# A new table of places for all operations, and ten dummy matmul groups instead of four, in a fused linear-attention and feed-forward kernel

## The chip, the cores and the metric

The kernel runs on one core of one Trainium2 chip. TensorE (PE) multiplies, VectorE (DVE) and ScalarE (ACT) do the elementwise work, GpSimd (POOL) a few reductions across partitions, and SyncE (SP) issues every DMA from one queue, in order. The metric is the device time of one execution in microseconds (us); a kernel's time is the median of several runs.

## The reference, cut to what matters

```python
# q, k, v: 8 x 8 x 576 x 64 (batch, heads, sequence, head width), float32
q_s = softmax(q, axis=-1)                  # over the 64 of a head
k_s = softmax(k, axis=2)                   # over the sequence
kv  = einsum('bhsd,bhse->bhde', k_s, v)    # 64 x 64 for each head
x   = einsum('bhsd,bhde->bhse', q_s, kv)   # -> 4608 tokens x 512
h   = x @ w_in                             # 512 x 2048
g   = h * sigmoid(1.702 * h)
out = g @ w_out                            # 2048 x 512
```

Everything is float32. The weights arrive as 64-bit words and are converted on the chip.

## The kernel before, in words

The 4608 tokens are cut into twelve blocks of 384. A block needs its slice of x: DVE and ACT form the two softmaxes (lines 577 to 612 for the keys, 709 to 732 for the queries), PE multiplies keys with values (`kv_pairs`, line 643), transposes the queries against an identity (`q_tr`, 753) and multiplies both (`x_pairs`, 825). ACT and DVE bring x from PSUM to SBUF. For block 0 PE itself helps to form the low part of x (line 799).

To keep float32 accuracy, every operand of the feed-forward part is split into a high and a low part, and every product is three matmuls: high by high, high by low, low by high. Blocks 0 and 1 do this plainly: `g1` (line 853, x by w_in) and `g2` (line 885, g by w_out). The later blocks go in pairs: x and w_in are cut into quarters, from which seven products (`product`, line 1251, six matmuls of 384 columns each) give the eight quarter products. The same is done for w_out in the last four pairs (`stream`, `still_part`, both with matmuls of 256 columns at line 1386, and `gather`, which adds up the pieces); the pair of blocks 2 and 3 uses `out_part` (line 1514).

SBUF doesn't hold all the weights in all their forms. In the first 130 us the kernel loads the raw weights (`load_w`, line 419), converts them (`conv_w`: ACT at 448 and 463, DVE at 452, 456 and 473), and stores the results to DRAM tensors (`dwi`, `dwo`, later `dsh`, `dsl`, `dwa`, `dwb`). From then on `refill` (line 925) brings them back, half a megabyte at a time, into a few buffers that are used again and again: a load can be issued once the last matmul that reads the old contents has run, and it must land before the first matmul that reads the new. Two buffers, called wi4 and wi5 in the code, hold `dsh` and `dsl` pieces in turn. Early on, some weight buffers hold keys, values and queries of batches 0 and 1 (`ek`, `ev`, `eq`, `en`), and the raw weights that belong there wait until these have been read.

What sets the order: each operation is given to a `Plan` with its engine, what it reads and writes, and a closure that emits it. The table `FIRST` (line 115) has one number for each operation, its place in one list of all of them; operations are handed out so that each engine keeps the order of that list, and the program's instructions stand on each engine in that order. An engine runs its instructions strictly in order, so an instruction whose input is late holds up all that stand behind it on that engine; the same is true of SP, where a load whose buffer isn't free holds up the loads behind it.

At line 1596 `warm` emits a dummy group: two matmuls of the identity with itself into PSUM bank 3. Their result is never read (bank 3 is overwritten with `start=True` by the next user). Each dummy group is an operation of its own in the plan, so the table sets where it stands. It needs nothing but the identity, the second load of SP's queue.

Of the kernel before, what the change touches and what calls it, by code (L numbers as in the profile page):

```python
# [17 lines left out]
class Plan:  # L18
# [277 lines left out]
def efficient_attention_then_gelu_ffn(  # L296
# [1259 lines left out]
    def at(rank, f, *a):  # L1556
        tasks.append((rank, len(tasks), f, a))
# [43 lines left out]
    for i in range(4):  # L1601
        at(-89.05 + 0.001 * i, lambda rank: plan.add("PE", 0.93, ("ident",), (("bank", 3),), rank, warm))
# [256 lines left out]
```

## Time and profile before

| | us |
|---|---|
| median of 3 runs | 864.79 (863.8 to 866.38) |
| the profiled execution | 859.32, with a span of 857.5 |
| PE busy | 809.0 (94%), of it weight loads beside matmuls 755.1 |
| DVE busy | 607.0 (71%) |
| ACT busy | 488.6 (57%) |
| mean granted clock of TensorE | 0.994 |

The span runs from the first to the last instruction; 1.8 us of the profiled execution lie around it. Matmuls are pipelined, and a matmul's record holds its latency too, so PE's busy share is high wherever matmuls follow each other: what one costs is read from start to start in a stretch without waits. DMA was moving 268 GB/s on average, and at its highest some 420 GB/s.

### The profile page before, as it was taken

What the parts mean: (1) busy time and instruction counts of PE and PEld (TensorE: products, weight loads), DVE (VectorE), ACT (ScalarE), POOL (GpSimd) and SP (SyncE); (2) the same over time, 40 slices, a digit from 0 to 9 for tenths busy, and PEclk for the clock granted to TensorE, in tenths of its full rate; (3) what the DMA queues carried; (4) which work ended last, traced back from release to release, by engine and by line L of the source; (5) the groups of instructions that cost most, each with busy time, mean ns of one, the idle gap of its engine ahead of it and who ended that gap; (6) DMA issues with size and microseconds to landing.
All of it is one profiled execution on the core that took longest, in us unless ns stands there. A gap on an engine that the chain in (4) does not pass through costs nothing.

```text
span 857.5 us, 14803 instructions
## 1 busy us (share of the span) xinstructions
PE 809.0 (94%) x5716; PEld 755.1 (88%) x5716; DVE 607.0 (71%) x1091; ACT 488.6 (57%) x897; POOL 22.7 (3%) x21
## 2 busy tenths in 40 slices
PE   3799999999989999999999899999999999999998
PEld 2688988788878888989999889899999999899997
DVE  7898768787778787766786756887656476444474
ACT  3886456465645676656565564676565465335452
POOL 1100010000000100000000100000000000000000
PEclk9899999999999999999999999999999999999999
DMA  9878976627898879797877679757776668676763
GB/s 359 348 301 293 419 309 247 223 75 274 270 352 289 292 277 341 259 357 241 299 255 272 218 239 354 274 186 254 253 238 223 225 228 302 244 258 233 272 225 143
DMA packets 83190, 229.79 MB, mean 268 GB/s; under 512 B 8240, under 2 KB 32944, under 8 KB 83120
## 3 DMA queue, kind: packets, MB, share of 16 engines
q1 hardware_dynamic: 83120, 228.85, 74.4%
q8 instruction: 45, 0.74, 0.3%
q14 instruction: 25, 0.20, 0.1%
HBM read 181.63 MB, written 47.19 MB: 267 GB/s over the span
## 4 chain that ended last, share of the span: by engine, by line
PE 68%; DMA 19%; DVE 8%; ACT 2%; SPq 1%; issue 1%; DVEq 0%; ACTq 0%
PE bank L1251 26%; PE bank L1386 21%; PE bank L885 6%; PE bank L853 6%; PE bank L1514 5%; DMA w<-dwo 3%; DMA w<-dwi 2%; PE bank L643 2%; DMA dwb<-sl 2%; DMA w<-dsl 2%; DMA w<-dwa 2%; PE bank L825 1%; DMA kt<-in_k 1%; DMA w<-dsh 1%; PE bank L753 1%
## 5 line engine op out<-in xcount | busy, mean ns | idle before, releaser
L1251 PE MATMUL bank<-xc,w 128*128 128x384 f32 x1680 | 317.7, 338 | 15.0 <-DVE g L1270 4.0
L1251 PEld LDWEIGHTS bank<-xc,w 128*128 128x128 f32 x1680 | 289.1, 188 | 23.1 <-DVE g L1270 5.0
L1386 PE MATMUL bank<-w,pu 128*128 128x256 f32 x1260 | 167.6, 283 | 2.9 <-DMA w<-dwo 2.9
L1386 PEld LDWEIGHTS bank<-w,pu 128*128 128x128 f32 x1260 | 159.5, 189 | 7.4 <-issue 4.5
L1386 PE MATMUL bank<-w,xc 128*128 128x256 f32 x756 | 101.8, 282 | 2.4 <-DMA w<-dwb 1.2
L1386 PEld LDWEIGHTS bank<-w,xc 128*128 128x128 f32 x756 | 95.6, 188 | 4.8 <-ACT work L1476 1.4
L853 PE MATMUL bank<-xh,w 128*128 128x384 f32 x256 | 71.1, 342 | 1.4 <-ACT g L859 1.4
L885 PE MATMUL bank<-w,gh 128*128 128x512 f32 x192 | 61.1, 399 | 0.0
L853 PEld LDWEIGHTS bank<-xh,w 128*128 128x128 f32 x256 | 47.5, 191 | 3.8 <-ACT g L859 1.9
L1293 ACT COPY g<-bank 128x384 f32<-128x384 f32 x52 | 24.9, 479 | 41.0 <-PE bank L1251 35.6
L853 PE MATMUL bank<-xl,w 128*128 128x384 f32 x128 | 43.5, 340 | 0.0
L1278 ACT ACTIVATE g<-bank 128x384 f32<-128x384 f32 x51 | 25.0, 490 | 28.7 <-PE bank L1251 25.8
L1293 ACT COPY bank<-bank 128x384 f32<-128x384 f32 x40 | 18.6, 465 | 39.4 <-PE bank L1251 39.3
L885 PEld LDWEIGHTS bank<-w,gh 128*128 128x128 f32 x192 | 34.9, 188 | 6.3 <-issue 0.9
L1270 DVE TENSOR_TENSOR g<-bank,g 128x384 f32<-128x384 f32 x33 | 18.4, 556 | 28.0 <-PE bank L1251 25.9
L885 PE MATMUL bank<-w,gl 128*128 128x512 f32 x96 | 37.9, 395 | 0.0
L1289 DVE TENSOR_TENSOR pu<-g,pu 128x384 fp32r<-128x384 f32 x47 | 25.9, 562 | 16.7 <-ACT pu L1286 16.5
L591 POOL PARTITION_ALL_REDUCE mx<-mx x16 | 22.0, 1394 | 524.4 <-DVE mx L587 515.4
L1289 DVE TENSOR_TENSOR xc<-g,xc 128x384 fp32r<-128x384 f32 x32 | 17.7, 554 | 18.3 <-ACT xc L1286 18.3
L1514 PE MATMUL bank<-w,gp 128*128 128x512 f32 x108 | 29.7, 395 | 0.0
L859 ACT ACTIVATE g<-bank 128x384 f32<-128x384 f32 x32 | 15.5, 492 | 23.1 <-PE bank L853 21.8
L1293 ACT COPY work<-bank 128x384 f32<-128x384 f32 x28 | 13.4, 478 | 25.6 <-PE bank L1251 21.3
(187 smaller groups left out, 1308.9 us busy)
## 6 DMA issues: line engine op xcount, KB each, us to landing
w<-dwo SPq DMA_DIRECT2D x48, 512.0 KB, 5.5
w<-dwb SPq DMA_DIRECT2D x48, 512.0 KB, 6.9
w<-dwi SPq DMA_DIRECT2D x44, 512.0 KB, 5.9
w<-dsh SPq DMA_DIRECT2D x32, 512.0 KB, 5.2
w<-dsl SPq DMA_DIRECT2D x32, 512.0 KB, 5.6
w<-dwa SPq DMA_DIRECT2D x32, 512.0 KB, 6.1
vt<-in_v SPq DMA_DIRECT2D x14, 650.0 KB, 8.3
kt<-in_k SPq DMA_DIRECT2D x14, 640.0 KB, 5.9
```

Of the source, the lines that this page charges most:

```text
L591: nc.gpsimd.partition_all_reduce(flat, flat, P, bass_isa.ReduceOp.max)
L643: nc.tensor.matmul(pk[r0 : r0 + D, m // 2, m % 2], kt[:, o + a, c, :], vt[:, o + a, c, :], start=c == 0, stop=c == CM - 1, tile_position=( ...
L853: nc.tensor.matmul(ph, wi[w][j][:, c, :], x[:, c, :], start=c == 0 and i == 0, stop=c == KC - 1 and i == 2,)
L859: nc.scalar.activation(gt, ph, AF.Gelu_apprx_sigmoid)
L885: nc.tensor.matmul(po[c], x[:, cs], wo[w][j], start=j == 0 and i == 0, stop=j == NJ - 1 and i == 2)
L1251: nc.tensor.matmul(pb, ws[w][:, c * P : (c + 1) * P], xx[x][:, c * TB : (c + 1) * TB], start=p in FRESH and c == 0 and i == 0, stop=c == 1 ...
L1270: lambda: nc.vector.tensor_tensor(out=d, in0=pb, in1=o, op=ALU.add),
L1278: lambda: nc.scalar.activation(d, src, AF.Gelu_apprx_sigmoid), table="gelu")
L1289: lambda: nc.vector.tensor_tensor(out=get()[1], in0=d, in1=get()[0].bitcast(F32), op=ALU.subtract),
L1293: plan.add("ACT", act(TB), (PB,), (key,), free_, lambda: nc.scalar.copy(dst, pb))
L1386: nc.tensor.matmul(po, y[:, cs], w, start=start and i == 0, stop=i == 2, skip_group_check=True,)
L1514: nc.tensor.matmul(po[:, f0:f1], x[:, cs], w[:, h * DM + f0 : h * DM + f1], start=m == 0 and e == 0 and i == 0, stop=m == NQ - 1 and e == ...
```

## The change

The table `FIRST` is replaced as a whole (3222 numbers instead of 3216), and the loop that adds dummy groups runs ten times instead of four. No operation of the real work is added, removed or altered: the numbers of real DMAs, DVE, ACT and POOL operations are the same.

```diff
 FIRST = [
-    1870, 1, 3, 65, 33, 49, 51, 52, 4, 2, 0, 10, 9, 7, 6, 12, 22, 15, 110, 19, 115, 5, 31, 27, 44, 40, 166, 37, 117,
...
+    622, 1, 3, 30, 10, 12, 14, 16, 19, 20, 44, 49, 51, 62, 4, 2, 0, 8, 11, 5, 7, 6, 25, 34, 48, 28, 59, 21, 38, 15,
...
 ]
@@ -1598,7 +1598,7 @@
         for _ in range(2):
             nc.tensor.matmul(bank[3][:, :P], ident, ident, start=True, stop=True)
 
-    for i in range(4):
+    for i in range(10):
         at(-89.05 + 0.001 * i, lambda rank: plan.add("PE", 0.93, ("ident",), (("bank", 3),), rank, warm))
```

The table's numbers tell a reader nothing; what they do is seen in the order of the instructions. First PE, from its first instruction on (L1599 are the dummy matmuls, two to a group; L753 the transposes of the first block's queries `en`; L643 keys by values of batch 0). Lines with - stand before, lines with + now:

```order
+L1599 MATMUL bank_66<-ident 128x128 x12
 L753 MATMUL bank_64<-ident,en_111 128x128 x3
-L1599 MATMUL bank_66<-ident 128x128 x2
-L643 MATMUL bank_69<-vt_96,kt_94 64x65 x20
 L753 MATMUL bank_63<-ident,en_111 128x128 x3
 L1599 MATMUL bank_66<-ident 128x128 x6
+L643 MATMUL bank_69<-vt_96,kt_94 64x65 x20
+L753 MATMUL bank_67<-ident,en_111 128x128 x3
+L1599 MATMUL bank_66<-ident 128x128 x2
 L753 MATMUL bank_66<-ident,en_111 128x128 x3
 L643 MATMUL bank_70<-vt_97,kt_95 64x65 x20
-L753 MATMUL bank_67<-ident,en_111 128x128 x3
```

Six dummy groups now stand ahead of everything on PE, three behind the first two transposes and one ahead of the last; before, one stood behind the first transpose and three behind the second.

Next DVE, some forty instructions in, up to the subtraction of the maxima from the keys of batch 1 (L605 on `ek_113`). L452, L456 and L473 convert weights, L711 and L715 begin the query softmax of block 1, L581 and L584 take maxima of keys:

```order
+L452 TENSOR_SCALAR raw<-raw 128x512 x2
+L581 TENSOR_TENSOR tmp_92<-ek_115 128x512
+L456 SCALAR_TENSOR_TENSOR work_84<-work_84,raw 128x512
+L605 TENSOR_TENSOR ek_113<-ek_113,mx_105 128x1280
 L456 SCALAR_TENSOR_TENSOR work_83<-work_83,raw 128x512
+L452 TENSOR_SCALAR raw<-raw 128x1024
+L473 TENSOR_TENSOR w<-work_84,w 128x512
+L456 SCALAR_TENSOR_TENSOR work_85<-work_85,raw 128x1024
+L584 TENSOR_TENSOR mx_104<-tmp_92 128x256
 L711 TENSOR_REDUCE qm_188<-eq_110 128x12
 L715 TENSOR_TENSOR eq_110<-eq_110,qm_188 128x768
-L605 TENSOR_TENSOR ek_113<-ek_113,mx_105 128x1280
```

The subtraction has moved ahead of one conversion and of the two steps of the query softmax.

Last SP, in the round of products that begins block 10's pair (some 720 us into the profiled execution). `w_530` before and `w_556` now are the buffers wi4 and wi5, `w_408` before is wi2 and wi3; `dsh0` and `dsl0` are first read by the same product. Before:

```order
L925 DMA w_530<-dsl0_157 128x1024
L925 DMA w_408<-dwi2_119 128x1024
L925 DMA w_530<-dsh0_149 128x1024
L1494 DMA out_0<-work0_83 128x2x256
```

And now:

```order
L925 DMA w_376<-dwi0_117 128x1024
L925 DMA w_722<-dwb4_181 128x1024
L925 DMA w_556<-dsh0_149 128x1024
L925 DMA w_556<-dsl0_157 128x1024
L925 DMA w_425<-dwi1_118 128x2x256
```

`dsh0` stood third and now stands ahead of `dsl0`; the load of `dwi2` no longer stands between the two.

At the start of SP's queue two loads of raw w_out go into buffers that hold keys and values of batch 1 until PE has read them. Before they stand 20th and 22nd, and behind them four loads of raw weights, a megabyte each, that wait for nothing of batch 1; now they stand 26th and 27th, behind those four.

## Rows read from the trace of the kernel before

**Rows 1.** Waits of PE, whole span: total us, times, longest.

```profile
PE bank L1251 <- DVE g L1270: 4.0, 2, 2.3
PE bank L1386 <- DMA w<-dwo: 3.1, 4, 1.2
PE bank L1251 <- DMA w<-dwi: 3.0, 5, 0.9
...
PE bank L1251 <- DMA w<-dsh: 2.8, 2, 1.6
...
PE bank L853 <- ACT g L859: 1.4, 1, 1.4
```

**Rows 2.** Timeline of PE, first 60 us: start, us, what, count, [idle before].

```profile
12.70 1.06 PE L1599 MATMUL bank<-ident 128*128 128x128 f32 x4
16.48 2.44 PE L643 MATMUL bank<-vt,kt 128*64 128x65 f32 x40 [2.73 <-ACT kt L610]
...
21.33 1.39 PE L643 MATMUL bank<-vt,kt 128*64 128x65 f32 x40
...
31.48 2.44 PE L643 MATMUL bank<-ev,ek 128*64 128x65 f32 x40 [2.70 <-ACT ek L610]
33.85 0.69 PE L853 MATMUL bank<-xh,w 128*128 128x384 f32 x1
```

**Rows 3.** Timeline of DVE, first 40 us.

```profile
18.97 0.16 DVE L651 TENSOR_SCALAR r<-bank 128x2 f32<-128x2 f32 x1 [1.51 <-PE bank L643]
...
20.57 0.69 DVE L581 TENSOR_TENSOR tmp<-ek 128x512 f32<-128x512 f32 x1
...
26.18 0.69 DVE L456 SCALAR_TENSOR_TENSOR work<-work,raw 128x512 int32<-128x512 int32 x1
26.78 0.95 DVE L711 TENSOR_REDUCE qm<-eq 128x12 f32<-128x768 f32 x1
27.76 0.96 DVE L715 TENSOR_TENSOR eq<-eq,qm 128x768 f32<-128x768 f32 x1
28.64 1.48 DVE L605 TENSOR_TENSOR ek<-ek,mx 128x1280 f32<-128x1280 f32 x1
```

**Rows 4.** DMA issues: the identity, once, KB, us to landing.

```profile
ident<-in_eye SPq DMA_DIRECT2D x1, 64.0 KB, 2.5
```

**Rows 5.** Stretches: busy of PE, PEld, DVE, ACT, POOL; PEclk, DMA share, GB/s.

```profile
30.00:32.00 2.00, 0.52 (x10) 0.52 (x12) 1.86 (x5) 1.84 (x3) 0.00 (x0) 0.50 1.01 406
32.00:34.00 2.00, 2.00 (x37) 1.88 (x33) 1.72 (x2) 1.24 (x3) 0.00 (x0) 0.50 0.23 90
...
36.00:38.00 2.00, 2.00 (x11) 2.00 (x10) 2.00 (x4) 1.20 (x3) 0.00 (x0) 0.84 0.99 403
...
48.00:50.00 2.00, 2.00 (x44) 1.74 (x43) 2.00 (x3) 1.94 (x4) 0.00 (x0) 1.00 0.00 0
```

**Rows 6.** Timeline of SP, first 60 us; the time includes SP's own waits.

```profile
17.99 16.34 SPq L419 DMA_DIRECT2D raw<-in_w_out  x2
...
36.14 13.77 SPq L419 DMA_DIRECT2D raw<-in_w_in  x2
```

**Rows 7.** Timeline of SP, 700 to 726 us.

```profile
716.59 0.42 SPq L925 DMA_DIRECT2D w<-dsh  x1
```

**Rows 8.** Timeline of PE, 712 to 726 us.

```profile
723.04 1.32 PE L1251 MATMUL bank<-xc,w 128*128 128x384 f32 x6 [1.57 <-DMA w<-dsh]
```

**Rows 9.** Chain of waits in order of time: start, us, what.

```profile
700.01 13.01 PE bank L1386 x108
...
776.49 2.09 PE bank L1251 x12
```

**Rows 10.** Timeline of DVE, 455 to 480 us.

```profile
471.24 0.95 DVE L711 TENSOR_REDUCE qm<-qt 128x12 f32<-128x768 f32 x1 [4.43 <-DMA qt<-in_q]
```

**Rows 11.** Timeline of SP, 440 to 480 us.

```profile
462.43 1.69 SPq L560 DMA_DIRECT2D qt<-in_q  x1
```

**Rows 12.** Stretch at 474 us, columns as in rows 5.

```profile
474.00:476.00 2.00, 2.00 (x6) 2.00 (x7) 1.43 (x3) 0.49 (x1) 0.00 (x0) 0.50 1.00 331
```

334 rows, old and new, of the table FIRST are left out of this document.

## The prediction

> **What bounds the kernel now.** I read the list of waits by engine first, then the first 70 us of each engine's timeline, then the stretches with the granted clock, and last the chain of waits. PE is the engine that sets the end: from 33.85 us, when the first feed-forward matmul starts [rows 2], it has work almost without a break, and what can be won is its waits. These fall into four kinds. First, the start: PE waits for the first softmaxed queries and then in pieces, 2.73 and 2.70 us among them [rows 2], because DVE has forty instructions to do in order and is nearly always busy. Second, weights that land late: 3.1 + 3.0 + 2.8 = 8.9 us over eleven waits for `dwo`, `dwi` and `dsh` [rows 1]. Third, 4.0 us for DVE's sums at line 1270 [rows 1], which are late when DVE itself stands at a load; the worst case is at 471 us, where DVE sits 4.43 us before a query reduction [rows 10] until the queries land, 8.8 us after their issue at 462.43 [rows 11], and behind it the clock is at its lower level, 1.2 GHz [rows 12]. Fourth, 1.4 us for ACT's gelu at 68 us [rows 1].
>
> **The start, without the dummies.** The first keys of batch 1 must be exponentiated before their product with the values (L643 on `ek`), which stands ahead of the first feed-forward matmul on PE in both orders. In the trace their subtraction on DVE runs from 28.64 [rows 3], the product at 31.48 after a wait of 2.70 for the exponential, the feed-forward at 33.85 [rows 2]. In the new order the subtraction stands ahead of L711 (from 26.78 to 27.76: 0.98), L715 (to 28.64: 0.88) and one L456 (26.18 to 26.78: 0.60); one L581 more stands before it (0.69) [rows 3]. Also, DVE waited 1.51 us at 18.97 for PE's first key product of batch 0 [rows 3]. In the new order the second half of the query softmax, the second key subtraction, a conversion of weights and a maximum stand before that instruction, some 5 us of work, and PE's product should be done by then. Sum: 0.98 + 0.88 + 0.60 + 1.51 - 0.69 = 3.3 us earlier. What is next in line there, ACT's copies and exponential, is moved up with it. I take -3.3; the ends are -4.0 (no wait of DVE left at all) and 0 (the weights of the first products aren't converted in time).
>
> **The dummies.** The identity takes 2.5 us to land [rows 4] and is asked for among the first, so PE can start on them at about 4 us. A group took 1.06 us at 12.7 us [rows 2]: six take 6.4 and end near 10.5. The first transposes, which ended before that dummy at 12.70, come later now, since one reduction and one maximum (0.95 + 0.69, as L711 and L581 [rows 3]) more stand ahead of their queries on DVE: the six groups are covered by that wait. Three groups (3.2 us) follow from 14.3 on and end near 17.5. The first key product of batch 0, at 16.48 in the trace [rows 2], waits for an exponential that comes 0.95 us later, at about 17.4. The last stands ahead of a transpose. So up to a microsecond or so may be added to it, but batch 0's second key product, which DVE's order holds back to about 20, hides that. Cost 0, the ends +1.6 and -1.0: the first key product took 2.44 us for 40 records where the second took 1.39 [rows 2], so at the higher clock it is 1.05 shorter.
>
> **The clock.** From 30 to 36 us it is at 0.50 [rows 5], PE having stood idle before 31.48 [rows 2]. It is up again within 36 to 38 (0.84 on average, so near 36.6); if it never fell, the 5.2 us from 31.48 on would take half, 2.6 less. But the dummies all stand before the fourth transpose, and the gap before batch 1's key product, with its exponential of 1.3 us on ACT, stays; I count nothing. The row before it needs care: batch 1's key product took 2.44 us at a clock of 0.50, and batch 0's first took the same 2.44 at 16.48 [rows 2], so PE was at 1.2 GHz there too. The Trainium skill (TensorE: Matmul & The Clock Gate, "What's actually happening") says that the throttled state is the default and that activity releases it, and idleness brings it back: by this rule dummies that end before 20 us hold nothing up at 30 us, and speak against a gain from them. The trace agrees, for it shows four dummy groups before 21 us and the low clock after 30. By the rule the term is 0; if the dummies did hold the clock it would be -2.6.
>
> **The raw weights.** SP stood 16.34 us from 17.99 on and 13.77 from 36.14 on [rows 6], for buffers that PE had not yet read; the DMA share was 0.23 at 32 to 34 us and 0.00 at 48 to 50 [rows 5]. In the new order the loads without such a need stand first. Counted by shape, 25 loads with 17.4 MB stand ahead of the first that waits for batch 1; at 406 GB/s [rows 5] they take 43 us, and PE has read that buffer at about 30. So DMA should not stand idle there, and the weights come up to 8 us sooner. PE was busy anyway, so only the wait at 68 us goes: -1.4 [rows 1], the ends -1.4 and 0.
>
> **Weights later on.** For each of the 260 weight loads that PE reads I counted along the order the matmuls from the moment SP can issue it (the last reader of its buffer, or that of a load ahead of it in the queue) to its first reader, at 13.01/108 = 0.120 us for the narrow and 2.09/12 = 0.174 us for the wide matmul [rows 9]. Loads with less than 7 us: 18 before, 14 now; the fifth with the shortest lead had up to 10.8 us, now up to 12.9. One example: `dsh0` was issued at 716.59 [rows 7] and PE went on at 723.04 after 1.57 of waiting [rows 8], 6.4 us after the issue. In the new order 54 narrow and 12 wide matmuls lie between, 54 x 0.120 + 12 x 0.174 = 8.6 us, and for `dsl0` 18 narrow fewer, 6.4. I take a third of the 8.9 us: -3.0; the ends -8.9 and +3 (a few leads became shorter, two of 4.2 us among them).
>
> **Loads that DVE reads.** By the same count, leads under 5 us: 31 of 105 before, 18 of 103 now. But at 471 us nothing is won: there 8.1 us of PE's work lie between the release of the query buffer and the sum that stands behind the reduction, in both orders. I take -1.0 of the 4.0; the ends -4.0 and 0.
>
> **New waits.** An order built anew has its own late spots, which no row of before can show. The old one left 4.0 + 8.9 + 1.4 = 14.3 us in rows 1 alone; I add +1.5, a tenth, the ends 0 and +10.
>
> **Sum.** -3.3 + 0 + 0 - 1.4 - 3.0 - 1.0 + 1.5 = -7.2 us. The profiled execution took 859.3 us (span 857.5 and 1.8 around it), which gives 852.1. The median of the three runs is 864.8, 5.5 more; a run without the profiler has this spread in late transfers, and longer leads should help there no less. The forecast for the median is 864.8 - 7.2 = 857.6.
>
> **Rivals.**
> (a) Only the start gains. The stages behind it lose as much in new spots as they win: -3.3 - 1.4 + 2.5 = -2.2, 862.6. For it: the sums of line 1270 hang on PE's own matmuls a few rows before, and those chains are as short now as before. Against: the counts of leads, which moved for nearly all loads.
> (b) Slower. The two loads of `dwo` and `dwa` whose lead is now 4.2 us, each at the end of a pair of blocks, land as late as the queries at 471 us, 8.8 us after the issue. Each then stops PE for 4.6 us, and the clock falls behind it as at 474 us, where two microseconds at half speed [rows 12] cost 1.0: 2 x 5.6 = 11.2, less the start's 4.7: +6.5, 871.3, with nothing won elsewhere. It decides from a landing of some 6.6 us on, where two waits of 2.4 us make the 4.7. For it: the two had 5.3 and 6.3 us before. Against: half-megabyte loads mostly take less, as `dsh0` with 6.4.
> (c) The dummies also hold the clock at 30 to 36 us: -7.2 - 2.6 = -9.8, 855.0. For it: ten groups are more than four; against it: the clock's row above.
> (d) The table doesn't do what the count says, since late transfers decide everything: no change, 864.8.
>
> **Chances and range.** Forecast 0.45, (a) 0.22, (b) 0.13, (c) 0.12, (d) 0.08. A change of under 0.3% (2.6 us) can't be told from none. Faster is the forecast but for 0.02 of its spread, (c), and half of (a), which lies at the bound: 0.43 + 0.12 + 0.11 = 0.66. Same is that 0.02, the other half of (a) and 0.07 of (d): 0.20. Slower is (b) and the last 0.01 of (d): 0.14. The forecast's own range is 853 to 862; with (a) and (c) and the open end of the new waits, 850.5 to 866.5 holds eight in ten, and leaves out (b) and the best ends.
>
> **What would show it.** Batch 1's first key product on PE at about 28 and the first feed-forward matmul near 30.5; no DMA share under 0.5 between 30 and 55 us; no wait of PE at line 853 at 60 to 75 us; the waits for `dwo`, `dwi` and `dsh` at 6 us or less in sum; the wait behind the query load near 470 still there; dummies done before the queries, the clock still at 0.50 somewhere between 25 and 36 us. The forecast is wrong if the first feed-forward matmul isn't 2 us earlier, or if PE's waits behind 60 us add up to more than before.

## The result and the profile after

The changed kernel takes 825.97 us (median; 825.61 to 826.8), the kernel before 865.59 (863.8 to 869.91): a ratio of 0.9537, with a 95% interval of 0.95 to 0.9573. The prediction was 857.6, so the direction was right and the size far too small. The profiled execution took 825.61 us, span 823.8, against 859.32 and 857.5. The two traces differ by 33.7 us; that is what the traces can explain, and the remaining 6 us of the difference of medians are there because the profiled execution of the kernel before was one of its shorter ones.

First the whole list of PE's waits in the changed kernel (line waited for: us in total, times, longest), which answers to [rows 1]:

```profile
PE bank L753 <- DVE en L731: 4.4, 1, 4.4
PE bank L1599 <- DMA ident<-in_eye: 4.0, 1, 4.0
PE bank L643 <- ACT ek L610: 2.5, 1, 2.5
PE bank L853 <- DVE w L473: 0.6, 1, 0.6
PE bank L753 <- ACT raw L777: 0.6, 1, 0.6
PE bank L825 <- DVE kvn L661: 0.4, 1, 0.4
PE bank L825 <- DVE work L1270: 0.3, 1, 0.3
```

All but the rows of 0.6 and 0.3 belong to the start. No load of weights is waited for any more, and only one wait for a sum of line 1270 is left (0.3, at L825). The same list of the kernel before had, beside [rows 1], some ten smaller groups behind the start that the prediction did not count, these among them:

```profile
PE bank L1251 <- ACT xc L1286: 1.9, 1, 1.9
...
PE bank L1386 <- DMA w<-dwb: 1.2, 1, 1.2
...
PE bank L1251 <- DMA w<-dsl: 1.1, 2, 0.7
PE bank L1386 <- DMA w<-dwa: 0.9, 1, 0.9
```

Summed behind the first feed-forward matmul, PE's idle time is 24.9 us before (12.2 ended by a load, the rest by DVE or ACT) and 1.7 after. Weight loads (PEld) that stood idle while the matmul ahead of them was still recorded are not in that sum; PEld's own idle time there fell by 29.2 us, from 52.9 to 23.7. With the 3.2 us of the start this makes 32.4 of the 33.7.

The start, on PE (start, us, what, [idle before]); it answers to [rows 2]:

```profile
3.99 5.23 PE L1599 MATMUL bank<-ident 128*128 128x128 f32 x24 [3.99 <-DMA ident<-in_eye]
...
17.63 2.03 PE L643 MATMUL bank<-vt,kt 128*64 128x65 f32 x40
...
28.76 2.00 PE L643 MATMUL bank<-ev,ek 128*64 128x65 f32 x40 [2.46 <-ACT ek L610]
30.69 0.69 PE L853 MATMUL bank<-xh,w 128*128 128x384 f32 x1
```

and on DVE, answering to [rows 3]:

```profile
20.57 0.15 DVE L651 TENSOR_SCALAR r<-bank 128x2 f32<-128x2 f32 x1
...
25.92 1.48 DVE L605 TENSOR_TENSOR ek<-ek,mx 128x1280 f32<-128x1280 f32 x1
```

The keys of batch 1 are subtracted 2.7 us sooner, DVE no longer stands idle ahead of L651, and the first feed-forward matmul starts at 30.69 instead of 33.85. Next the same four stretches as [rows 5]: no gap is left in the traffic of the raw weights, and the low clock is shorter.

```profile
30.00:32.00 2.00, 2.00 (x19) 1.88 (x17) 1.97 (x4) 1.57 (x2) 0.00 (x0) 0.50 1.03 417
32.00:34.00 2.00, 2.00 (x12) 2.00 (x11) 2.00 (x3) 1.42 (x3) 0.00 (x0) 0.82 1.01 406
...
36.00:38.00 2.00, 2.00 (x14) 2.00 (x13) 1.86 (x5) 1.42 (x3) 0.70 (x1) 1.00 1.02 401
...
48.00:50.00 2.00, 1.47 (x8) 1.48 (x9) 1.94 (x5) 2.00 (x5) 0.00 (x0) 1.00 1.03 414
```

The gain then grows through the whole span. The first L1251 starts 4.6 us sooner (176.3 against 180.9), the 505th (368 against 381) 13, the 841st (495 against 515) 20, the 1345th (686 against 713) 27, the last L1386 34. So it is not one place; the kernel before lost a little at many.

### The profile page after: what moved, and what is told of

It is laid out like the page before. It is cut to its first block, busy times and chain, and to the rows that moved or that the text cites. A ratio compares the mean times of both kernels' runs of the same rounds, so it can differ in the third digit from the quotient of the medians.

```text
span 823.8 us, 14925 instructions
## 1 busy us (share of the span) xinstructions
PE 807.6 (98%) x5740; PEld 758.9 (92%) x5740; DVE 607.9 (74%) x1091; ACT 488.7 (59%) x895; POOL 24.0 (3%) x21
## 4 chain that ended last, share of the span: by engine, by line
PE 92%; DVE 6%; DMA 1%; issue 0%; SPq 0%; ACT 0%; DVEq 0%
PE bank L1251 35%; PE bank L1386 29%; PE bank L1514 8%; PE bank L885 7%; PE bank L853 7%; PE bank L825 2%; PE bank L643 2%; PE bank L753 2%; DVE work L456 1%; DMA dwb<-sl 1%; DMA eq<-in_q 1%; DVE w L473 1%; DVE kvn L661 1%; DVE raw L452 0%; DVE en L731 0%; DVE eq L715 0%
## 5 line engine op out<-in xcount | busy, mean ns | idle before, releaser
L1251 PE MATMUL bank<-xc,w 128*128 128x384 f32 x1680 | 312.6, 336 | 0.0
L1251 PEld LDWEIGHTS bank<-xc,w 128*128 128x128 f32 x1680 | 289.1, 188 | 3.6 <-ACT bank L1293 0.6
L1386 PE MATMUL bank<-w,pu 128*128 128x256 f32 x1260 | 167.5, 282 | 0.0
L1386 PEld LDWEIGHTS bank<-w,pu 128*128 128x128 f32 x1260 | 159.1, 189 | 3.9 <-issue 3.8
L1386 PE MATMUL bank<-w,xc 128*128 128x256 f32 x756 | 101.7, 281 | 0.0
L1386 PEld LDWEIGHTS bank<-w,xc 128*128 128x128 f32 x756 | 95.7, 188 | 1.4 <-issue 1.2
L853 PE MATMUL bank<-xh,w 128*128 128x384 f32 x256 | 70.7, 342 | 0.6 <-DVE w L473 0.6
L853 PEld LDWEIGHTS bank<-xh,w 128*128 128x128 f32 x256 | 47.3, 190 | 3.5 <-DVE w L473 0.9
L853 PE MATMUL bank<-xl,w 128*128 128x384 f32 x128 | 43.3, 338 | 0.0
L1289 DVE TENSOR_TENSOR pu<-g,pu 128x384 fp32r<-128x384 f32 x47 | 25.7, 555 | 10.9 <-ACT pu L1286 10.4
L760 ACT COPY qT<-bank 128x384 f32<-128x384 f32 x40 | 18.7, 482 | 18.8 <-PE bank L753 18.8
L1270 DVE TENSOR_TENSOR work<-bank,work 128x384 f32<-128x384 f32 x16 | 8.9, 557 | 28.2 <-PE bank L1251 21.3
```

The source lines that it names most:

```text
L760: (nc.vector.tensor_copy if 4 <= t < 6 else nc.scalar.copy)(qT, pq[:, :TB])
L853: nc.tensor.matmul(ph, wi[w][j][:, c, :], x[:, c, :], start=c == 0 and i == 0, stop=c == KC - 1 and i == 2,)
L1251: nc.tensor.matmul(pb, ws[w][:, c * P : (c + 1) * P], xx[x][:, c * TB : (c + 1) * TB], start=p in FRESH and c == 0 and i == 0, stop=c == 1 ...
L1270: lambda: nc.vector.tensor_tensor(out=d, in0=pb, in1=o, op=ALU.add),
L1289: lambda: nc.vector.tensor_tensor(out=get()[1], in0=d, in1=get()[0].bitcast(F32), op=ALU.subtract),
L1386: nc.tensor.matmul(po, y[:, cs], w, start=start and i == 0, stop=i == 2, skip_group_check=True,)
```

## The experiments

Their tables are written in fewer lines, so their line numbers lie 4 to 8 below those above (L745 is L753, L1243 is L1251, L1378 is L1386).

**Four dummies** (`four_dummies`) and **ten dummies** (`ten_dummies`). The new table without the six leading groups, and the old one with them:

```diff
-    for i in range(10):
+    for i in range(4):
```

> The new order with the six leading dummy groups left out, four kept. Theory (the order does it all, the dummies sit in a wait): within 1.5 us of the changed kernel's 826, and the first feed-forward matmul near 30.7 us as with ten. Rival (the dummies hold the clock): 2 to 4 us slower, 828 to 830, with more of the stretch before 36 us at a granted clock of 0.50.

> The old order with six more dummy groups at its head, ten in all. Theory (the order does it all): 864 to 867, no difference from the kernel before. Rival (the dummies hold the clock): 861 to 863, and the 0.50 that the kernel before shows from 30 to 36.6 us is gone or shorter.

Measured: four dummies with the new order 826.62 us (ratio to before 0.9566, 0.9518 to 0.9613), ten with the old order 868.38 (1.0038, 1.0002 to 1.0075). So the dummies give nothing. Two expectations missed: ten with the old order lies a little above the 864 to 867 given, and with four the first feed-forward matmul comes a microsecond sooner still, here in PE's timeline and in the stretch with the clock:

```profile
28.33 1.39 PE L635 MATMUL bank<-ev,ek 128*64 128x65 f32 x40 [2.45 <-ACT ek L602]
29.65 0.57 PE L845 MATMUL bank<-xh,w 128*128 128x384 f32 x1
```

```profile
30.00:32.00 2.00, 2.00 (x8) 2.00 (x8) 1.97 (x3) 1.57 (x2) 0.00 (x0) 0.50 1.01 408
```

The low clock at 30 us is there with four dummies as with ten. Earlier the six leading groups even work against their purpose: in the changed kernel they end at 9.2 us, PE then stands idle for 4.4 us, and the granted clock is 0.50 from 14 to 18 us, through the transposes and the groups behind them; with four it is 1.00 from 16 to 18. In all nine traces with ten groups the clock falls to 0.50 between 10.9 and 12.8 us. By the end of the plain blocks the two differ by 0.4 us only (last L853 at 170.1 and 170.5). With ten in the old order the stretch is still slow:

```profile
34.00:36.00 2.00, 2.00 (x28) 1.88 (x27) 1.64 (x5) 1.24 (x4) 0.00 (x0) 0.50 0.00 0
```

**One part of the list new, the other old** (`new_then_old`, `old_then_new`). All operations that stand ahead of the first L1251 in one list, in that list's order, and behind them the others in the other list's order:

```
FIRST of new_then_old: new list up to its first L1251, then what is left in the old list's order
FIRST of old_then_new: old list up to its first L1251, then what is left in the new list's order
```

> The new list up to the first seven-product matmul (L1251, at about 180 us), the old one behind it. Theory (the gain is spread over the whole span, 4.7 us of it ahead of that point as the two traces' landmarks show): 865.6 - 4.7 = 861, from 858 to 863. Rival (the first part sets up all the rest, a schedule won at the start is kept): under 845.

> The old list up to the first seven-product matmul (L1251), the new one behind it. Theory (the gain is spread over the span, 29 of the 33.7 us lie behind that point): 826 + 5 = 831, from 829 to 835. Rival (the first part sets up the rest): over 850.

Measured: 863.03 us (0.997, 0.9935 to 1.0006) and 834.69 (0.9658, 0.9609 to 0.9706). The first, just outside the 858 to 863 expected, can't be told from no change; the second keeps most of the gain. So the gain lies where the order is new; a good start does not carry over, nor does a bad one spoil the rest. The second is 8.7 us above the changed kernel, 4 more than the landmarks gave; its first L1251 starts at 182.3, 6.0 later than in the changed kernel.

**The queue of loads alone, the compute alone** (`old_loads`, `new_loads`). For `old_loads` PE, DVE, ACT and POOL keep the new list, and SP's entries stand in the old one's order; for `new_loads` the other way round:

```
FIRST of old_loads: PE, DVE, ACT, POOL as in the new list; SP as in the old one
FIRST of new_loads: PE, DVE, ACT, POOL as in the old list; SP as in the new one
```

> PE, DVE, ACT and POOL in the new order, SP's queue in the old one (29 of its 518 entries stand up to ten places elsewhere, where the old place would wait for itself). Theory (what counts is how the queue of loads fits the order of their readers, so a queue made for another order brings the waits back): over 855, PE's waits for loads and for sums that are late behind a load at 15 us or more. Rival 1 (the order of the compute is the gain, the queue incidental): under 835. Rival 2 (each gives its part): 840 to 850.

> PE, DVE, ACT and POOL in the old order, SP's queue in the new one (16 of its 518 entries stand up to ten places elsewhere). Theory (queue and readers must fit): over 855. Rival 1 (the order of the compute is the gain): over 860. Rival 2 (the queue alone is the gain, its loads issued earlier): under 840.

Measured: 998.82 us (1.1502, 1.1426 to 1.1578) and 944.08 (1.0882, 1.082 to 1.0943). Neither half is better by itself: each with the other's partner is far worse than either kernel, and by much more than I had expected. PE's waits in `old_loads`:

```profile
PE bank L1243 <- DMA w<-dwi: 29.6, 5, 8.6
PE bank L1243 <- DMA w<-dsh: 16.8, 6, 4.8
PE bank L1378 <- DMA w<-dwa: 15.7, 2, 12.2
```

**Every refill half as large** (`half_before`, `half_after`, and `old_loads_half` on the misfit):

```diff
+            to, of = (x[..., : x.shape[-1] // 2] for x in (to, of))
             nc.sync.dma_start(out=to, in_=of)
```

> The kernel before with every refill (L925) of half its bytes, the other half of each weight buffer left as it was, so the products are made with stale weights in part. Theory (loads that land after their need are the loss, straight on PE 12 us and through DVE and ACT as much again): shorter transfers land in time, 840 to 850, and PE's waits for weights fall from 12 us to under 3. Rival (the order of the compute is the loss, loads incidental): over 858.

> The changed kernel with every refill of half its bytes, as in the run before. Theory (its loads land in time already): 824 to 827, no gain. Rival (PE's matmuls are slowed by the traffic beside them): under 822.

> The new compute with the old queue of loads (999 us), every refill of half its bytes, stale weights in part. Theory (the misfit's loss is mostly the queue's order: a load behind one whose buffer isn't free yet can't be issued, however small it is): over 900. Rival (it is transfer time, as in the kernel before): under 860.

Measured: the kernel before falls to 835.14 us (0.963, 0.9578 to 0.9682), more than expected; the changed kernel stays at 825.83 (0.9519, 0.9467 to 0.957); the misfit falls from 998.82 to 940.77 (1.0862, 1.0825 to 1.0899). In the kernel before a refill now lands in 3.4 to 3.9 us (5.2 to 6.9 before), and of its waits behind the start these are the two largest that are left:

```profile
PE bank L817 <- ACT qT L752: 1.5, 2, 1.3
...
PE bank L1244 <- DMA w<-dsh: 1.3, 1, 1.3
```

PE's idle time behind the first feed-forward matmul falls from 24.9 to 5.4 us, and not only the part that a load ended: what DVE and ACT ended falls from 12.7 to 4.1, because they too stand at transfers less (DVE 38.5 to 21.6 us behind that matmul, of it 13.6 and 4.5 at stores). So 33 of the 42 us between the kernel before (868.11 beside these runs) and the changed kernel (825.83 with half refills, 825.97 with whole ones) go with half the bytes, with the old order left as it is: they are transfers that landed after their need. In the misfit they are only 58 of the 173 us that it lies above the changed kernel; the rest stays with transfers of half the size. That the rest is the queue's order, a load that must wait for its buffer holding all behind it, was the expectation that held, but no run shows it by itself.

**One query load** (`one_query`). Two entries of the old queue moved, at the place of [rows 10, 11]:

```
before: dsl1, store, dwb4, dsl2, dwb4, dwi3, q (half of block 9), ...
now:    dsl1, store, dwb4, dwi3, q, dwb4, dsl2, ...
```

> The kernel before with two entries of SP's queue moved: ahead of the query load that landed 8.8 us after its issue near 462 us, two loads of half a megabyte (dwb4, dsl2) now stand behind it and behind the last load of dwi. Theory (a load lands when the bytes queued ahead of it are through): 1.05 MB less ahead of it at 400 GB/s, so it lands 2.6 us sooner, some 6 us after its issue; DVE's wait there falls from 4.4 to under 2.5, and PE's wait for the sum behind it from 2.3 to under 0.5. The time moves by 2 to 4 us, within the scatter of the kernel before. Rival (this load is late by itself, however little is ahead): it lands at 8 us or more again and the two waits stay.

Here is SP's queue right ahead of that load in the kernel before, the last four of six transfers (start, us, what; its time includes SP's own waits):

```profile
459.65 0.42 SPq L925 DMA_DIRECT2D w<-dwb  x1
460.17 0.44 SPq L925 DMA_DIRECT2D w<-dsl  x1
460.67 0.42 SPq L925 DMA_DIRECT2D w<-dwb  x1
461.14 1.20 SPq L925 DMA_DIRECT2D w<-dwi  x1
```

and in this run:

```profile
466.06 0.42 SPq L917 DMA_DIRECT2D w<-dwb  x1
466.54 0.53 SPq L917 DMA_DIRECT2D w<-dwi  x1
467.88 0.33 SPq L552 DMA_DIRECT2D qt<-in_q  x1
468.25 0.95 SPq L917 DMA_DIRECT2D w<-dwb  x1
469.24 0.43 SPq L917 DMA_DIRECT2D w<-dsl  x1
```

The query load landed 5.13 us after its issue, where it took 8.78 before (8.95 and 9.34 in `new_then_old` and `ten_dummies`, whose order is the same there). The issue is the start of SP's row, and that row itself took 0.33 us here and 1.69 before [rows 11]; from the row's end to the landing it is 4.8 and 7.1 us, so 2.3 of the 3.7 us are the landing itself, where 2.6 were expected. DVE's reduction follows without a wait:

```profile
473.14 0.95 DVE L703 TENSOR_REDUCE qm<-qt 128x12 f32<-128x768 f32 x1
```

On PE the 36 wide matmuls of this place took 10.93 us before, from 465.15 to 476.08:

```profile
465.15 4.32 PE L1251 MATMUL bank<-xc,w 128*128 128x384 f32 x24
470.38 1.28 PE L1251 MATMUL bank<-xc,w 128*128 128x384 f32 x6 [0.91 <-DMA w<-dwi]
473.99 2.29 PE L1251 MATMUL bank<-xc,w 128*128 128x384 f32 x6 [2.33 <-DVE g L1270]
476.08 1.99 PE L1386 MATMUL bank<-w,pu 128*128 128x256 f32 x12
```

and 6.25 now, without a gap, from 471.56 to 477.81:

```profile
471.56 6.41 PE L1243 MATMUL bank<-xc,w 128*128 128x384 f32 x36
477.81 1.60 PE L1378 MATMUL bank<-w,pu 128*128 128x256 f32 x12
```

That is 4.7 us at this place from two moved loads, where I had written that nothing could be won. The whole time is 859.89 us (0.9956, 0.9911 to 1.0001), in line with it, but by itself not told from no change.

**A little more traffic** (`quarter_after`, `quarter_before`). A copy of 128 KB within DRAM ahead of every refill:

```diff
+            nx[0] += 1
+            nc.sync.dma_start(out=dx[nx[0] % 8], in_=dw[src][:, : DM // 2])
             nc.sync.dma_start(out=to, in_=of)
```

> The changed kernel with an added copy from DRAM to DRAM, a quarter as large as a refill, issued ahead of every refill. Theory (the new order fits the landing times with about a microsecond to spare at many loads, so it is lost when they all come a little later): 6 to 25 us slower than the changed kernel, with waits for loads on PE again. Rival (it has leads long enough for such a delay): within 2 us of 826.

> The same added copies in the kernel before. Theory (its loads are late already, each delay falls on PE in full): 15 to 40 us slower than the kernel before, more than the changed kernel loses. Rival (its time isn't set by when loads land): within 5 us.

Measured: 845.59 us (0.978 of the kernel before, 0.9738 to 0.9822) and 919.85 (1.0621, 1.057 to 1.0671). The changed kernel loses 20 us, the kernel before 54, more than I gave it. In the changed kernel the waits for loads are back:

```profile
PE bank L1247 <- DMA w<-dsl: 2.5, 2, 1.7
...
PE bank L1382 <- DMA w<-dwo: 1.9, 3, 0.8
```

So the new order has no large reserve: it fits the landing times as they are, and copies of a quarter of each refill's bytes cost it half of its gain.

## Why the prediction was right in direction and wrong in size

**The start: right.** Taken at -3.3, measured -3.16 (30.69 for 33.85 [rows 2]), through the steps that were named, but with some luck in the size: the subtraction came 2.7 sooner instead of 3.3, DVE's idle time at L651 gone, and the other 0.4 is batch 1's key product, 2.00 us long for 2.44, for which I had counted nothing.

**The dummies: right.** Taken at 0; the whole time shows 0.65 us between four and ten, under what can be told. At the place itself they cost 1.0 us, within the end of +1.6 that I had put beside them, and the first key product took 2.03 us with ten and 1.39 with four, so the hoped-for faster clock there came without them.

**The clock: right that the dummies don't hold it.** Still at 0.50 from 30 us on, and with four dummies too; rival (c) falls. It is 0.82 in the stretch from 32 to 34 us and 1.00 from 36 to 38, where [rows 5] showed 0.50 and 0.84, so the low stretch is shorter, by the new order and not by the dummies; the term of 0 had left that out.

**The raw weights: right.** DMA share 1.02 and 1.03 where it was 0.99 and 0.00; the wait at 68 us [rows 1] is gone, a new one of 0.6 (for a conversion at 48.5) is there.

**"Weights later on": this is the step that failed.** I took a third of 8.9 us, -3.0. All of it went, with the 3.2 us of `dwb`, `dsl` and `dwa` that I had left out: 12.2 us to nothing. The measure was wrong, not only the fraction. I counted the time from issue to first reader and called under 7 us short; 18 such loads became 14, so I expected little. In the two traces, as far as the semaphores tell, that count hardly moves either: 42 of 242 loads that PE waits on are read less than 7 us after their issue before, 39 of 235 after. But of all the readers 28 started within 0.2 us of the landing before, and 7 after. So one fixed lead does not tell late from in time, because the landing itself goes with what SP has issued ahead. Of the half-megabyte refills in the trace before, the 24 issued with nothing else under way landed after 3.2 to 4.4 us, the 74 with more than 1.8 MB under way after 5.0 to 10.5. Those whose reader came within 0.2 us of the landing had on average 1.5 MB under way before (23 refills), and 0.6 now (5). Over all refills with leads under 7 us it is 0.9 MB before and after, so the new order doesn't empty the queue; that it gives the loads with short leads little to stand behind is argued from this, and tested for one load alone (`one_query`). Two loads of rival (b), on SP and on PE in the changed kernel, had little lead and nothing issued just ahead of them:

```profile
540.89 0.32 SPq L925 DMA_DIRECT2D w<-dwo  x1
...
785.38 0.32 SPq L925 DMA_DIRECT2D w<-dwa  x1
```

```profile
543.81 4.37 PE L1386 MATMUL bank<-w,pu 128*128 128x256 f32 x35
...
789.51 3.73 PE L1386 MATMUL bank<-w,pu 128*128 128x256 f32 x29
```

SP had issued nothing for 4.4 and 8.3 us ahead of them; they landed after 3.8 and 4.1 us, their readers came at 544.76 and 789.51, and PE's matmuls had no gap, though with under 0.1 us between landing and reader nothing was to spare. The rival had given them 8.8 us because one query load took that. The Trainium skill (DMA: Bandwidth & Descriptors, "Anatomy of one DMA") puts a transfer at about 2.0 us plus its bytes over 436 GB/s; an estimate from that page is 3.2 us for half a megabyte alone in the queue, and it states the formula for GpSimd's path, while these are SP's. The trace goes that way: 3.8 and 4.1 us behind a pause in the queue, 5.2 to 6.9 as the median of all.

**"Loads that DVE reads": failed in the same way.** I took -1.0 of 4.0 and wrote that at 471 us nothing could be won, since 8.1 us of PE's work stood against a landing of 8.8. The place is there in the changed kernel, and the load takes 6.16 us, so that DVE's reduction starts on time. SP's row first, then DVE's and PE's:

```profile
447.36 0.34 SPq L560 DMA_DIRECT2D qt<-in_q  x1
```

```profile
453.54 0.95 DVE L711 TENSOR_REDUCE qm<-qt 128x12 f32<-128x768 f32 x1
```

```profile
451.05 6.41 PE L1251 MATMUL bank<-xc,w 128*128 128x384 f32 x36
```

I had treated 8.8 us as this load's own time, and it counted SP's row of 1.69 us as well. It stood behind 2.5 MB issued in some 5 us, and `one_query` took 3.7 us off it with two moves; in the changed kernel the four loads of the 5 us ahead of it are 1.8 MB. Behind the first feed-forward matmul DVE stood 38.5 us at transfers (24.9 at loads, 13.6 at stores) and now 7.4. That this is why the sums of line 1270 and ACT's results come in time as well fits `half_before`, where both fell together.

**New waits: about right, by luck.** Taken at +1.5, a tenth that no row gave; 1.7 us is all that is left behind the first feed-forward matmul, and 0.6 of it (L753 for `raw`) stood in the list before too.

**The sum.** With the waits as they turned out, its own terms would be -3.2 for the start and -29.2 for what PE and its weight loads waited behind it: 827 for the profiled execution, which took 825.61. Of that I had counted 14.3 us [rows 1], left the many rows of about 1 us aside, and granted 5.4 (1.4 + 3.0 + 1.0), less 1.5 for new waits. The rest, about a microsecond, I can only argue: behind 60 us the clock was at 0.50 for 3.4 us before and not at all now.

What stays open: `half_before` lies 9 us above the changed kernel, of which the start explains 4.9 (its first feed-forward matmul is at 35.6 us) and 3.7 of idle time nearly all the rest; which moves in the order bring that was not tried.

## What to carry to other kernels

Where one queue feeds all loads, as here, a load's time from issue to landing isn't a property of the load (3.2 to 10.5 us for the same half megabyte): look at the bytes still under way when it is issued, and compare the landing that goes with them with its reader's time. Make transfers smaller once, as an experiment with stale data: it shows in one run how much of a kernel's time is late landing, before any order is searched. And an order of loads is worth only as much as it fits the order of its readers: change both together or neither.

## What the hardware showed that I had not expected

A wait costs PE more than its length. Behind some waits the granted clock is at 0.50 for a while, and over the runs the time at 0.50 grows with the idle time, though not in proportion. Idle time is PE's behind the first feed-forward matmul, low clock is the time at 0.50 between 60 us and the end of the span, rest is what is left of the span behind that matmul when the idle time is taken off; all in us:

| run | idle | low clock | rest |
|---|---|---|---|
| changed kernel | 1.7 | 0.0 | 791.4 |
| `half_before` | 5.4 | 0.0 | 792.5 |
| before | 24.9 | 3.4 | 798.7 |
| `new_then_old` | 26.7 | 14.5 | 804.0 |
| `quarter_before` | 61.0 | 47.8 | 820.6 |
| `new_loads` | 83.6 | 85.9 | 821.1 |
| `old_loads` | 129.1 | 126.3 | 838.7 |

In `old_loads` the same work takes 47 us longer than in the changed kernel, beside its 129 us of waiting. Not all of that is the clock: some 12 of the 47 us are idle time of the weight loads that the matmuls' records hide, and so are about 6 of the 7 us of the kernel before. At about the same idle time the profiled execution of the kernel before had 3.4 us at the low clock and `new_then_old` 14.5, with 5 us more for the rest; so waits of about the same sum bring the clock down more in one execution than in another. It goes with the whole time too: of the runs of the kernel before made beside the experiments, those with a mean granted clock of 0.993 or more took 855.09 to 862.75 us, those with 0.988 or less 865.75 to 873.28. The profiled execution, 859.3 us at 0.994, is one of the first kind. Whether the clock makes those runs long or their longer waits make the clock low, these numbers don't tell.

Late transfers also show as scatter: all runs of the kernel before lie between 855.09 and 873.28 us, those of the changed kernel between 825.61 and 826.8, and with half refills those of the kernel before between 834.69 and 836.47.
